# Attention and bilinear layers in split float32 on one core: the token-order softmax by VectorE block transposes and small DMAs in place of TensorE transposes, reads one batch later, state rows last

## The chip, the cores and the metric

The kernel runs on one core of a Trainium2 chip. The metric is the device time of one execution in microseconds. Before the change it is 510.85 us, the median of three runs (510.68 to 511.10). The engines are named as in the profile: PE is TensorE, DVE is VectorE, ACT is ScalarE, POOL is GpSimd, SP is SyncE (here it only issues DMAs).

## The reference, cut to what matters

```python
# x: 8 batches, 8 heads, 512 tokens, 64;  state: 8, 8, 32, 64
a  = softmax(x @ state.T / 8)          # each token over the 32 state rows
xread = a @ state
a2 = softmax(state @ x.T / 8)          # each state row over the 512 tokens
sread = a2 @ x
rows = concat(xread, sread)            # 544 rows a batch, 4352 in all, 512 wide
out = ((rows @ w1) * (rows @ w2)) @ w3 @ w_out
```

All of it is float32; the four weights come as float64. The layers have 1024 hidden columns.

## The kernel before, in words

**Precision.** A float32 operand of the large products is split into a rounded part and a remainder (`split`, lines 94 to 99: ACT writes `hi`, DVE subtracts and writes `lo`). A product is then three matmuls: hi by lo, hi by hi, lo by hi.

**Algebra.** w3 and w_out are multiplied once, in the prologue, to `wo` (line 85), eight column blocks (four in `w34_first`, 367, while the weights arrive; four in `w34(i)`, 379), each split by `finish(i)` (361). The token rows need no xread: the weights are multiplied with the state of a batch ("sets": `sw_steps`, 247; `sw_quarter`, 259, for batch 0), and stage 1 (281 to 295) multiplies these with the softmax `at`. Stage 1 has eight tiles `ft` of 128 hidden columns, 12 matmuls each; `hidden` (271) multiplies its two halves and splits the product into `g_hi` and `g_lo`. Stage 2 (304) multiplies g with `wo` for four token tiles `tt` of 128, 24 matmuls each, and `store` (312) copies the sum (ACT) and sends it out on ACT's DMA queue. Batch 0 does a part of stage 2 in between (`early_stage2`, 397).

**Softmax.** `attention_steps(b)` (160) has three parts. `scores` (164) computes `state @ x.T` in PSUM, 128 partitions by 1024; DVE transposes it in 32x32 blocks (172) and normalises over the state (to 202), and a second block transpose (206) gives `at`, which is split (208). The other softmax, over tokens, is the exponential `e2` (180 to 184) with its sums. `transpose_a2` (210) turns `e2` into token order with eight 128x128 transposes on PE (215) and a copy by ACT (217). `read_state` (219) multiplies that with the tokens `x_s` (64 matmuls by the profile's count, 227), DVE scales (232), and POOL's DMAs collect the rows in `sread` (237).

**Order.** PE's and SP's work runs as it is written; ACT's and DVE's is written by hand in the prologue up to `order.close()` (439), and set by a scheduler behind it. During the stage 2 of batch b stand the side steps of batch b+1 (`side_steps`, 319; `batch_stage2`, 342): scores and two sets behind the first token tile; transposes, two sets, reads and the rest of the softmax behind the second. Then `load_x(b + 2)` (145) loads state, `x_d` and the tokens `x_s`, the latter two into one buffer each. PSUM has two single banks for stage 2 and three pairs (`two_banks`, 91) for all else. At the start of batch 7 `state_rows` (480) does both stages for the 256 state rows, after `transpose_reads` (468) put `sread` into place during the last stage 2 of batch 6; the output of a state-row tile goes in four DMAs of 32 rows (501). A DMA from SP or ACT signals one of eight counters in turn, and waits until the DMA that had this counter before has landed.

Of the kernel before, what the change touches and what calls it, by code (L numbers as in the profile page):

```python
# [33 lines left out]
AHEAD = 2  # L34
PARTS = {0: (640, 1024), 1: (512, 1024)}
# [3 lines left out]
def attn_bilinear_kernel(  # L39
# [93 lines left out]
    x_tiles, sts = {}, {}  # L133
# [11 lines left out]
    def load_x(b):  # L145
        sts[b] = att.tile([P, NP, NS], F32, name="st")
        nc.sync.dma_start(out=sts[b], in_=st[b])
        x_tiles[b] = [
            att.tile([P, NP, S], F32, name="x_d", bufs=1), att.tile([P, NT, H, D], F32, name="x_s", bufs=1)
        ]  # L150
        for t, src in zip(x_tiles[b], (x_d, x_s)):
            nc.sync.dma_start(out=t, in_=src[b])
# [7 lines left out]
    def attention_steps(b):  # L160
        xd = x_tiles[b][0]
        a2 = {}

        def scores():
# [43 lines left out]
            split(*at_tiles[b], at)  # L208

        def transpose_a2():  # L210
            ps = two_banks()
            for kt in range(KT):
                for t in range(NT):
                    ts = slice(t * P, (t + 1) * P)
                    nc.tensor.transpose(out=ps[:, kt, ts], in_=a2["e"][:, kt, ts], identity=ident)  # L215
            a2["t"] = work_tile() if b < 2 else late.tile([P, KT, S], F32, name="a2_t")
            nc.scalar.copy(out=a2["t"], in_=ps)

        def read_state():

            xs = x_tiles[b][1]
# [19 lines left out]
        return scores, transpose_a2, read_state, a2  # L241
# [76 lines left out]

    def side_steps(b):

        if b == B:
            return [[]] * NT
        scores, transpose_a2, read_state, a2 = attention_steps(b)
        w = sw_steps(b)
        if b < 2:
            return [[scores, w[0], w[1]], [w[2], w[3], transpose_a2], [read_state], []]
        softmax = scores()
        first = partial(islice, softmax, 3)

        def rest():  # L330

            with tc.issue_after(a2["read"].ins):
                yield from softmax

        return [[first, w[0], w[1]], [transpose_a2, w[2], w[3], read_state, rest], [], []]
# [6 lines left out]
    def batch_stage2(b, gs):  # L342
        side = side_steps(b + 1)
        for tt in range(NT):

            between = transpose_reads if b == B - 2 and tt == NT - 1 else None
            stage2(gs, tt, [(out[b, tt * P:(tt + 1) * P], 0, P)], between)
            run(side[tt])
        if b + 2 < B:
# [3 lines left out]
    with tc.tile_pool(name="pro", bufs=2) as pro:  # L353
# [25 lines left out]
        def w34(i):  # L379
            w34_ps[i] = bank()  # L380
            for k in range(FT):
# [31 lines left out]
        scores, transpose_a2, read_state, _ = attention_steps(0)  # L413
        softmax = scores()
        next(softmax)
        for i in range(FT // 2):
            finish(i)
# [10 lines left out]
        transpose_a2()  # L428
# [127 lines left out]
```

## Time and profile before

| | |
|---|---|
| median of three runs | 510.85 us |
| profiled execution | 512.03 us |
| its span (first to last instruction) | 510.0 us |
| granted TensorE clock | 1.000 |
| transposes of the token softmax on PE (L215) | 64, 8.4 us busy |
| ACT copies behind them (L217) | 8, 1.01 us each |
| DMA, mean over the span | 95 GB/s |

The span is what the views divide; the profiled execution is 2.03 us longer than its span. A PE matmul of 128 by 512 is given with 390 to 397 ns, but matmuls overlap: a step from one to the next is 0.23 us. The chain of waits merges pieces of one engine and line, and so shows how long a group holds PE.

### The profile page before, as it was taken

What the parts mean: (1) busy time and instruction counts of PE and PEld (TensorE: products, weight loads), DVE (VectorE), ACT (ScalarE), POOL (GpSimd) and SP (SyncE); (2) the same over time, 40 slices, a digit from 0 to 9 for tenths busy, and PEclk for the clock granted to TensorE, in tenths of its full rate; (3) what the DMA queues carried; (4) which work ended last, traced back from release to release, by engine and by line L of the source; (5) the groups of instructions that cost most, each with busy time, mean ns of one, the idle gap of its engine ahead of it and who ended that gap; (6) DMA issues with size and microseconds to landing.
All of it is one profiled execution on the core that took longest, in us unless ns stands there. A gap on an engine that the chain in (4) does not pass through costs nothing.

```text
span 510.0 us, 7598 instructions
## 1 busy us (share of the span) xinstructions
PE 502.6 (99%) x3222; PEld 375.4 (74%) x3222; DVE 269.7 (53%) x370; ACT 227.6 (45%) x341; POOL 16.5 (3%) x38
## 2 busy tenths in 40 slices
PE   8999999999999999999999999999999999999997
PEld 6434457867876887688778867886788679998885
DVE  4669885466439253915391449154915583732510
ACT  6667784344436243624362435243524463632410
POOL 0000001001000100010001000000100010000000
PEclk9999999999999999999999999999999999999999
DMA  8997672032104300420042013201410001001001
GB/s 331 339 394 283 262 297 89 6 125 81 54 1 134 124 2 1 142 117 1 14 140 105 0 32 140 89 1 31 155 68 1 21 26 44 1 6 37 2 34 49
DMA packets 12386, 48.20 MB, mean 95 GB/s; under 512 B 1856, under 2 KB 3392, under 8 KB 7744
## 3 DMA queue, kind: packets, MB, share of 16 engines
q1 hardware_dynamic: 6336, 38.28, 20.6%
q10 hardware_dynamic: 4992, 8.92, 4.7%
q0 software_dynamic: 1024, 0.53, 0.4%
q8 instruction: 25, 0.41, 0.3%
q14 instruction: 9, 0.07, 0.1%
HBM read 38.27 MB, written 8.91 MB: 93 GB/s over the span
## 4 chain that ended last, share of the span: by engine, by line
PE 85%; DMA 6%; ACT 4%; DVE 3%; issue 1%; ACTq 0%; DVEq 0%
PE ps_o L300 37%; PE ps L290 34%; PE ps L141 7%; PE ps L494 5%; DMA raw<-in_w_k_dram 4%; ACT ulps L120 2%; PE ps L227 2%; DMA raw<-in_w3t_dram 1%; DMA raw<-in_w_dram 1%; PE ps L215 1%; ACT w_sb L117 1%; DVE wo_lo L98 1%; DVE w L128 0%; ACT w L117 0%; ACT wo_hi L97 0%
## 5 line engine op out<-in xcount | busy, mean ns | idle before, releaser
L300 PE MATMUL ps_o<-wo_lo,g_hi 128*128 128x512 f32 x272 | 107.9, 397 | 0.0
L300 PE MATMUL ps_o<-wo_hi,g_lo 128*128 128x512 f32 x272 | 106.1, 390 | 0.0
L300 PE MATMUL ps_o<-wo_hi,g_hi 128*128 128x512 f32 x272 | 105.9, 389 | 0.0
L275 DVE TENSOR_TENSOR tmp<-tmp,ps 128x512 f32<-128x512 f32 (+1 forms) x72 | 47.3, 656 | 107.4 <-ACT tmp L274 107.4
L290 PE MATMUL ps<-at_lo,sw_hi 128*128 128x512 f32 x256 | 100.1, 391 | 0.6 <-DVE sw_lo L98 0.6
L290 PE MATMUL ps<-at_hi,sw_hi 128*128 128x512 f32 x256 | 99.6, 389 | 0.0
L290 PE MATMUL ps<-at_hi,sw_lo 128*128 128x512 f32 x256 | 99.6, 389 | 0.0
L274 ACT COPY tmp<-ps 128x512 f32<-128x512 f32 (+1 forms) x72 | 40.5, 563 | 67.8 <-PE ps L290 66.9
L98 DVE TENSOR_TENSOR g_lo<-tmp,g_hi 128x512 fp32r<-128x512 f32 (+1 forms) x72 | 47.7, 662 | 42.8 <-ACT g_hi L97 42.7
L97 ACT CAST g_hi<-tmp 128x512 fp32r<-128x512 f32 (+1 forms) x72 | 42.9, 596 | 48.5 <-DVE tmp L275 48.4
L300 PEld LDWEIGHTS ps_o<-wo_lo,g_hi 128*128 128x128 f32 x272 | 51.0, 188 | 17.3 <-issue 6.7
L300 PEld LDWEIGHTS ps_o<-wo_hi,g_lo 128*128 128x128 f32 x272 | 51.1, 188 | 10.9
L315 ACT COPY tmp<-ps_o 128x512 f32<-128x512 f32 x34 | 20.0, 588 | 87.3 <-PE ps_o L300 87.3
L300 PEld LDWEIGHTS ps_o<-wo_hi,g_hi 128*128 128x128 f32 x272 | 51.1, 188 | 10.1
L290 PEld LDWEIGHTS ps<-at_lo,sw_hi 128*128 128x128 f32 x256 | 48.0, 188 | 11.5 <-DVE sw_lo L98 1.0
L290 PEld LDWEIGHTS ps<-at_hi,sw_lo 128*128 128x128 f32 x256 | 48.1, 188 | 10.0
L290 PEld LDWEIGHTS ps<-at_hi,sw_hi 128*128 128x128 f32 x256 | 48.1, 188 | 9.8
L98 DVE TENSOR_TENSOR sw_lo<-ps,sw_hi 128x1024 fp32r<-128x1024 f32 (+1 forms) x36 | 38.8, 1099 | 1.3 <-ACT sw_hi L97 0.2
L97 ACT CAST sw_hi<-ps 128x1024 fp32r<-128x1024 f32 (+1 forms) x36 | 32.2, 920 | 8.4 <-PE ps L141 8.3
L141 PE MATMUL ps<-w_sb,st 64*32 64x512 f32 (+1 forms) x576 | 31.5, 546 | 0.0
L237 POOL DMA_DIRECT2D sread<-scaled x32 | 15.8, 502 | 403.7 <-DVE scaled L232 403.7
L382 PE MATMUL ps_o<-w_sb,w 128*128 128x512 f32 x64 | 28.3, 597 | 0.5 <-DVE w L128 0.3
(65 smaller groups left out, 442.1 us busy)
## 6 DMA issues: line engine op xcount, KB each, us to landing
raw<-in_w_k_dram SPq DMA_DIRECT2D x8, 1024.0 KB, 6.9
x_d<-in_x_d_dram SPq DMA_DIRECT2D x8, 1024.0 KB, 5.4
x_s<-in_x_s_dram SPq DMA_DIRECT2D x8, 1024.0 KB, 5.7
raw<-in_w_dram SPq DMA_DIRECT2D x8, 1024.0 KB, 6.7
out_dram<-tmp ACTq DMA_DIRECT2D x32, 256.0 KB, 2.0
raw<-in_w3t_dram SPq DMA_DIRECT2D x4, 1024.0 KB, 7.5
st<-in_st_dram SPq DMA_DIRECT2D x8, 64.0 KB, 6.0
sread<-scaled POOLq DMA_DIRECT2D x32, 16.0 KB, 3.1
```

The source lines that it names most:

```text
L97: nc.scalar.copy(out=hi, in_=src),
L98: nc.vector.tensor_tensor(out=lo, in0=src, in1=hi.bitcast(F32), op=ALU.subtract),
L120: nc.scalar.activation(out=ulps[:, part], in_=low.bitcast(U32), func=AF.Copy, scale=2.0**-29)
L141: nc.tensor.matmul(ps[j * NS:(j + 1) * NS, q], sts[b][rows, j], moving(rows, j), start=True, stop=True)
L237: nc.gpsimd.dma_start(out=sread[rows, b // PER, j * KT:(j + 1) * KT], in_=scaled[j * NS:(j + 1) * NS])
L274: nc.scalar.copy(out=a_sb[:, :n], in_=ps[:, 0, :n])
L275: nc.vector.tensor_tensor(out=a_sb[:, :n], in0=a_sb[:, :n], in1=ps[:, 1, :n], op=ALU.mult)
L290: nc.tensor.matmul(ps[:, i], w[:, kt, c:c + P], a[:, kt], start=(k == 0), stop=(k == 3 * KT - 1))
L300: nc.tensor.matmul(ps[:, :DO], g, wo[w][:, ft, :], start=(ft == 0 and k == 0), stop=(ft == FT - 1 and k == 2))
L315: nc.scalar.copy(out=o, in_=ps[:, :DO])
L382: nc.tensor.matmul(w34_ps[i][:, :DO], w3s[i][:, k * P:(k + 1) * P], w_out[k], start=(k == 0), stop=(k == FT - 1))
L494: nc.tensor.matmul(ps[:, i, :n], w[:, ks], a, start=(k == 0), stop=(k == 3 * NP - 1))
```

## The change

The token softmax gets to token order without PE. At the end of the softmax (now a fourth part of `scores`) DVE transposes `e2` in 32x32 blocks, after the split of `at`, and SP issues 16 DMAs that put the blocks in their places: each takes 32 partitions, eight pieces of 32 numbers each. PE's eight transposes and ACT's copy go. The reads of batch b are done with the side steps of batch b+1 (those of batch 7 behind the first token tile of its own stage 2), and the tokens are loaded by a function of their own, `load_tokens`, at the end of the stage 2 before that. `transpose_reads` moves into the last stage 2 of batch 7, and the state rows behind everything. In the prologue, the columns 2 and 3 of w3 w_out are split in one piece; batch 0's tokens are loaded behind the third and fourth half of the weights; the second set stands inside the last column block of w3 w_out (five of eight matmuls before it, `LAST`, and three behind); and the scores of batch 1 come in the third quarter of batch 0's stage 1.

```diff
     def load_x(b):
...
-        x_tiles[b] = [
-            att.tile([P, NP, S], F32, name="x_d", bufs=1), att.tile([P, NT, H, D], F32, name="x_s", bufs=1)
-        ]
-        for t, src in zip(x_tiles[b], (x_d, x_s)):
-            nc.sync.dma_start(out=t, in_=src[b])
+        x_tiles[b] = att.tile([P, NP, S], F32, name="x_d", bufs=1)
+        nc.sync.dma_start(out=x_tiles[b], in_=x_d[b])
+
+    def load_tokens(b):
+        token_tiles[b] = att.tile([P, NT, H, D], F32, name="x_s", bufs=1)
+        nc.sync.dma_start(out=token_tiles[b], in_=x_s[b])
...
-            split(*at_tiles[b], at)
-
-        def transpose_a2():
-            ps = two_banks()
-            for kt in range(KT):
-                for t in range(NT):
-                    ts = slice(t * P, (t + 1) * P)
-                    nc.tensor.transpose(out=ps[:, kt, ts], in_=a2["e"][:, kt, ts], identity=ident)
+            last = split(*at_tiles[b], at)
+            yield
+
+            blocks = work_tile()
+            with tc.issue_after(last[1].ins):
+                nc.vector.transpose(out=flat(blocks), in_=flat(e2))
             a2["t"] = work_tile() if b < 2 else late.tile([P, KT, S], F32, name="a2_t")
-            nc.scalar.copy(out=a2["t"], in_=ps)
+            tiles = lambda t: t.rearrange("p k (t m) -> p (k t) m", m=P)
+            for j in range(NP):
+                for c in range(P // NS):
+                    mine, its = slice(j * NS, (j + 1) * NS), slice(c * NS, (c + 1) * NS)
+                    nc.sync.dma_start(out=tiles(a2["t"])[its, :, mine], in_=tiles(blocks)[mine, :, its])
...
         if b == B:
-            return [[]] * NT
-        scores, transpose_a2, read_state, a2 = attention_steps(b)
+            return [[reads[b - 1]], [], [], []]
+        scores, reads[b], a2 = attention_steps(b)
...
-        return [[first, w[0], w[1]], [transpose_a2, w[2], w[3], read_state, rest], [], []]
+        if b == 1:
+            return [[first], [reads[0], w[0], w[1]], [w[2], w[3], lambda: softmax], []]
+        return [[first, w[0], w[1]], [w[2], w[3], reads[b - 1], lambda: softmax], [], []]
...
-            between = transpose_reads if b == B - 2 and tt == NT - 1 else None
+            between = transpose_reads if b == B - 1 and tt == NT - 1 else None
...
+        if b + 1 < B:
+            load_tokens(b + 1)
         if b + 2 < B:
             load_x(b + 2)
...
-        for i in range(FT // 2):
-            finish(i)
+        finish(0)
+        finish(1)
+        split(wo["hi"][:, 2:4], wo["lo"][:, 2:4], pair[:, :, :DO])
...
-        transpose_a2()
...
+        load_tokens(0)
         w34(6)
         sets(0)
         finish(6)
-        w34(7)
+        w34(7, range(LAST))
+        sets(1)
+        w34(7, range(LAST, FT))
         finish(7)
-        sets(1)
...
-                load_x(1)
                 side = side_steps(1)
+            elif quarter == 2:
+                run(side.pop(0))
             stage1(0, 2 * quarter + 1, gs)
             if quarter == 0:
                 run([partial(convert_half, n) for n in range(4, 2 * QT)])
-                read_state()
-        run(side[0][1:] + side[0][:1])
+                load_x(1)
+                with tc.issue_after(last_split[1].ins):
+                    go(softmax)
+        run(side[0])
...
     for b in range(1, B):
-        if b == B - 1:
-            with tc.issue_after(last_split[0].ins), tc.issue_after(last_split[1].ins):
-                state_rows()
...
+    with tc.issue_after(last_split[0].ins), tc.issue_after(last_split[1].ins):
+        state_rows()
```

How the instructions stand, at three places. PE, the side steps of batch 3 behind the second token tile of batch 2 (L300 is stage 2, L215 the transposes, L141 a set, L227 the reads), before:

```order
L300 MATMUL ps_o<-wo_hi,g_lo 128x512
L215 MATMUL ps_1651<-ident,e_1582 128x128 x8
L141 MATMUL ps_1662<-w_sb,st 32x512 x8
L141 MATMUL ps_1675<-w_sb,st 32x512 x8
L227 MATMUL ps_1688<-x_s,a_t 32x64 x32
L300 MATMUL ps_o<-wo_lo,g_hi 128x512
```

And PE at the same place now (the lines are those of the changed kernel: L304 is stage 2, L142 a set, L231 the reads):

```order
L304 MATMUL ps_o<-wo_hi,g_lo 128x512
L142 MATMUL ps_1632<-w_sb,st 32x512 x8
L142 MATMUL ps_1645<-w_sb,st 32x512 x8
L231 MATMUL ps_1658<-x_s,a_t 32x64 x32
L304 MATMUL ps_o<-wo_lo,g_hi 128x512
```

The transposes are gone; the reads stand where they stood, but are those of batch 2. SP, from the last weights to the loads for batch 2, before:

```order
L113 DMA raw<-in_w_dram 128x1024 x6
L147 DMA st<-in_st_dram 128x128
L152 DMA x_d<-in_x_d_dram 128x2048
L152 DMA x_s<-in_x_s_dram 128x2048
L147 DMA st<-in_st_dram 128x128
```

And SP there now (L221 are the small DMAs, of batch 0 and batch 1 in one row):

```order
L114 DMA raw<-in_w_dram 128x1024 x2
L154 DMA x_s<-in_x_s_dram 128x2048
L114 DMA raw<-in_w_dram 128x1024 x4
L148 DMA st<-in_st_dram 128x128
L150 DMA x_d<-in_x_d_dram 128x2048
L221 DMA work<-work 32x8x32 x32
L154 DMA x_s<-in_x_s_dram 128x2048
```

Batch 0's tokens have moved behind two of the last six weight loads, and 32 small DMAs stand ahead of the tokens of batch 1. PE in the prologue, from the third column block of w3 w_out that is made there to stage 1 (L382 is w3 w_out, L290 stage 1), before:

```order
L215 MATMUL ps_317<-ident,e_271 128x128 x8
L382 MATMUL ps_o<-w_sb,w_260 128x512 x8
L141 MATMUL ps_365<-w_sb,st 32x256 x8
L141 MATMUL ps_378<-w_sb,st 32x256 x8
L382 MATMUL ps_o<-w_sb,w_332 128x512 x8
L141 MATMUL ps_402<-w_sb,st 32x256 x8
L141 MATMUL ps_413<-w_sb,st 32x256 x8
L290 MATMUL ps_425<-at_lo,sw_hi 128x512
```

And PE there now (L386 is w3 w_out, L294 stage 1):

```order
L386 MATMUL ps_o<-w_sb,w_256 128x512 x8
L142 MATMUL ps_352<-w_sb,st 32x256 x8
L142 MATMUL ps_365<-w_sb,st 32x256 x8
L386 MATMUL ps_o<-w_sb,w_317 128x512 x5
L142 MATMUL ps_384<-w_sb,st 32x256 x8
L142 MATMUL ps_395<-w_sb,st 32x256 x8
L386 MATMUL ps_o<-w_sb,w_317 128x512 x3
L294 MATMUL ps_412<-at_lo,sw_hi 128x512
```

The second set (ps_402 and ps_413, now ps_384 and ps_395) stands three matmuls earlier, inside the last column block.

More of the change, by code (lines that the diff above doesn't have):

```diff
@@ L34 @@
 AHEAD = 2
+LAST = 5
 PARTS = {0: (640, 1024), 1: (512, 1024)}
@@ L130, in to_f32 @@
                     )
-    x_tiles, sts = {}, {}
+    x_tiles, token_tiles, sts = {}, {}, {}
     def per_head(ps, b, moving):
@@ L160, in attention_steps @@
     def attention_steps(b):
-        xd = x_tiles[b][0]
+        xd = x_tiles[b]
         a2 = {}
@@ L239, in read_state @@
                 )
-        return scores, transpose_a2, read_state, a2
+        return scores, read_state, a2
     def sw_pair():
@@ L317, in store @@
             nc.scalar.dma_start(out=dest, in_=o[first:first + n])
+    reads = {}
     def side_steps(b):
         if b == B:
-            return [[]] * NT
-        scores, transpose_a2, read_state, a2 = attention_steps(b)
+            return [[reads[b - 1]], [], [], []]
+        scores, reads[b], a2 = attention_steps(b)
         w = sw_steps(b)
-        if b < 2:
-            return [[scores, w[0], w[1]], [w[2], w[3], transpose_a2], [read_state], []]
         softmax = scores()
         first = partial(islice, softmax, 3)
-        def rest():
-            with tc.issue_after(a2["read"].ins):
-                yield from softmax
-        return [[first, w[0], w[1]], [transpose_a2, w[2], w[3], read_state, rest], [], []]
+        if b == 1:
+            return [[first], [reads[0], w[0], w[1]], [w[2], w[3], lambda: softmax], []]
+        return [[first, w[0], w[1]], [w[2], w[3], reads[b - 1], lambda: softmax], [], []]
     def run(steps):
@@ L377, in convert_w3, with w34 @@
             return to_f32(pro, w3t[i - FT // 2], w3s[i])
-        def w34(i):
-            w34_ps[i] = bank()
-            for k in range(FT):
+        def w34(i, ks=range(FT)):
+            if ks[0] == 0:
+                w34_ps[i] = bank()
+            for k in ks:
                 nc.tensor.matmul(
@@ L412, in attn_bilinear_kernel @@
         load_x(0)
-        scores, transpose_a2, read_state, _ = attention_steps(0)
+        scores, reads[0], _ = attention_steps(0)
         softmax = scores()
         next(softmax)
-        for i in range(FT // 2):
-            finish(i)
+        finish(0)
+        finish(1)
+        split(wo["hi"][:, 2:4], wo["lo"][:, 2:4], pair[:, :, :DO])
         w34(4)
@@ L461, in attn_bilinear_kernel @@
                 run(side[tt - 1])
+        load_tokens(1)
         load_x(2)
```

2 lines of the change are left out of this document (1 added, 1 removed).

## The prediction

> **What bounds the kernel now.** The page's engine line and the shares of the chain that ended last come first: whose time is the span's time?
>
> ```profile
> PE 502.6 (99%) x3222; PEld 375.4 (74%) x3222; DVE 269.7 (53%) x370; ACT 227.6 (45%) x341; POOL 16.5 (3%) x38
> PE 85%; DMA 6%; ACT 4%; DVE 3%; issue 1%; ACTq 0%; DVEq 0%
> ```
>
> TensorE (PE) carries 85% of the chain; DMA, ScalarE and VectorE hold the other 14%, so I look where those lie. The view that gives busy time by stage (columns: length of the stage, then busy time of each engine) says it for the prologue, one batch in the middle and the tail.
>
> ```profile
> core 0: us, PE busy (x) PEld busy (x) DVE busy (x) ACT busy (x) POOL busy (x), PEclk, DMA share, GB/s
> 37.60:69.00 31.40, 31.02 (x136) 13.82 (x136) 28.52 (x37) 23.82 (x29) 0.00 (x0) 1.00 0.77 286
> 69.00:80.72 11.72, 11.15 (x141) 8.02 (x133) 9.53 (x15) 9.09 (x14) 0.89 (x2) 1.00 0.69 254
> 225.78:276.30 50.52, 50.52 (x345) 39.04 (x345) 26.04 (x34) 20.30 (x31) 1.97 (x4) 1.00 0.19 66
> 506.25:510.00 3.75, 0.00 (x0) 0.00 (x0) 0.00 (x0) 0.59 (x1) 0.00 (x0) 1.00 0.18 70
> ```
>
> In a middle batch PE is busy for 50.52 of 50.52 us, at full clock, while VectorE (DVE) is busy for 26.0 and ScalarE (ACT) for 20.3. So from the end of the prologue on, a microsecond taken off PE comes off the time, unless another engine then is late. In the prologue (37.6 to 69) DVE has 28.5 us of work in 31.4, as tight as PE. The tail is 3.75 us in which PE does nothing.
>
> **Term 1: the transposes on PE.** The chain in order of time (start, length, what) lists them in every batch; first, third and last of the seven after batch 0, with their neighbours in the third.
>
> ```profile
> 116.95 1.02 PE ps L215 x8
> ...
> 205.19 5.68 PE ps_o L300 x24
> 210.87 0.87 PE ps L215 x8
> 211.74 1.88 PE ps L141 x32
> 213.62 1.03 PE ps L227 x64
> 214.65 11.13 PE ps_o L300 x48
> ...
> 412.97 0.87 PE ps L215 x8
> ```
>
> The pieces follow without a gap, and the next piece is PE's in any case, so removing eight transposes removes their 0.87 us. Six batches give 5.22 and batch 1 gives 1.02: **6.24 us off**. All eight reads of the state remain, at 1.03 us each, and only change places; the pieces that begin alone after a switch of shape are as many as before (reads of batches 0 and 1 stood alone, now the scores of batch 1 and the reads of batch 7), so moving them costs nothing net.
>
> The transposes come at 109 ns each here (0.87 over 8). The Trainium skill ("TensorE: Matmul & The Clock Gate", Part 4: PE-mode transpose) gives about 275 ns for one in a kernel's context, and the page "VectorE: DVE Perf Modes" (The three transpose paths, and its rules) says to keep 128x128 transposes on TensorE. By 275 ns the estimate for 56 transposes would be 15.4 us off; the chain's row decides for 6.24.
>
> **What must take their place.** DVE does one more block transpose a batch, ACT one copy less.
>
> ```profile
> L206 DVE STREAM_TRANSPOSE work<-work 128x1024 f32<-128x1024 f32 x8 | 9.9, 1236 | 0.0
> L217 ACT COPY a_t<-ps 128x1024 f32<-128x1024 f32 x6 | 6.1, 1012 | 2.5 <-PE ps L215 2.5
> 218.73 1.23 DVE L98 TENSOR_TENSOR at_lo<-work,at_hi 128x1024 fp32r<-128x1024 f32 x1 [1.11 <-ACT at_hi L97]
> 229.15 0.69 DVE L275 TENSOR_TENSOR tmp<-tmp,ps 128x512 f32<-128x512 f32 x1 [9.20 <-ACT tmp L274]
> ```
>
> The new transpose has the form of L206, 1.24 us, and stands right behind the at_lo split; the last two rows show that DVE then idles for 9.2 us. It is covered eightfold; without that cover it would be 1.24 us a batch.
>
> Behind it SP issues 16 DMAs of 32 partitions x 8 pieces of 128 bytes (32 KB each). No row shows such a DMA. The nearest:
>
> ```profile
> 214.71 0.33 SPq L152 DMA_DIRECT2D x_s<-in_x_s_dram  x1
> 215.09 0.42 SPq L147 DMA_DIRECT2D st<-in_st_dram  x1
> sread<-scaled POOLq DMA_DIRECT2D x32, 16.0 KB, 3.1
> out_dram<-tmp ACTq DMA_DIRECT2D x8, 64.0 KB, 1.7
> ```
>
> SP issues one per 0.38 us (214.71 to 215.09), so 16 take 6.1 us; the landing lies between 1.7 us (rows of 2 KB) and 3.1 us (rows of 512 bytes). I take 3.1, nearest in size of piece: all 16 are in after 6.1 + 3.1 = **9.2 us**. The lower end is 7.8; the upper end is that they don't overlap at all, 16 x 3.1 = 50.
>
> Who waits? The reads, on PE, come a batch later, some 40 us on: no wait. The loads behind them on SP (tokens, then the next x_d) are needed a batch later too. Two places are closer.
> - Batch 0: its 16 DMAs read the work buffer into which DVE puts the scores of batch 1. DVE, and with it the splits that stage 1 needs, stands behind that wait. The pieces of PE between lengths it can hide in:
>
> ```profile
> 80.72 2.94 PE ps_o L300 x12
> 83.66 5.44 PE ps L290 x24
> 89.10 1.02 PE ps L141 x32
> 90.13 2.94 PE ps_o L300 x12
> ```
>
>  These four, 12.34 us, and 0.87 for the scores give 13.2 us from the last split of the first quarter to the scores; 1.24 goes to the block transpose, leaving 12.0. PE itself stalls only when the scores' PSUM buffer is wanted again, three tiles of stage 1 later; since the softmax needs most of that, I allow 1 us for it: **13 us against 9.2**, so nothing. If it takes the 50 us of the upper end, 37.
> - Every batch: the output DMA of the fourth token tile, on ACT, takes a completion counter that the fifth small DMA held, and ACT's first copy of the next stage 1 (L274, for which DVE waits in the last row of the softmax above) is behind it. The fifth is due 5 x 0.38 + 3.1 = 5 us after 221.2, at 226.2, about when that output is ready. A tile of stage 1 is 2.72 us (the 24 matmuls in 5.44 above are two tiles), and with three PSUM pairs the fourth tile wants the first one's back at 225.78 - 0.87 + 8.16 = 233.1; less a copy and a product, ACT must go on by 231.5. So PE would notice only from 10 us on. Nothing again.
>
> **Term 2: the prologue.** The pieces of it that end last, on PE, DVE and ACT:
>
> ```profile
> 38.86 0.59 ACT L97 CAST wo_hi<-ps 128x512 fp32r<-128x512 f32 x1 [1.64 <-DVE wo_lo L98]
> 39.47 0.69 DVE L98 TENSOR_TENSOR wo_lo<-ps,wo_hi 128x512 fp32r<-128x512 f32 x1 [0.65 <-ACT wo_hi L97]
> 40.08 1.24 DVE L172 STREAM_TRANSPOSE work<-ps 128x1024 f32<-128x1024 f32 x1
> 41.18 1.15 ACT L117 ACTIVATE w_sb<-raw 128x1024 f32<-128x1024 f32 x1 [1.73 <-DMA raw<-in_w_dram]
> 51.52 1.04 PE L215 MATMUL ps<-ident,e 128*128 128x128 f32 x8
> 52.85 1.12 PE L382 MATMUL ps_o<-w_sb,w 128*128 128x512 f32 x2 [0.30 <-DVE w L128]
> 71.66 0.39 PE L290 MATMUL ps<-at_hi,sw_lo 128*128 128x512 f32 x1
> 72.61 0.50 PE L290 MATMUL ps<-at_lo,sw_hi 128*128 128x512 f32 x1 [0.57 <-DVE sw_lo L98]
> 74.15 1.14 ACT L117 ACTIVATE w_sb<-raw 128x1024 f32<-128x1024 f32 x1 [1.13 <-DMA raw<-in_w_dram]
> ```
>
> The transposes of batch 0 (1.04 us) are worth nothing by themselves: after them PE waits 0.30 us more for the converted w3 from DVE. What moves that conversion is the split of w3 w_out's columns 2 and 3. It was two pairs with a wait between (ACT 1.64, DVE 0.65 idle); in one piece of 1024 the subtraction starts at once, at 38.14, and with the 1.23 of the at_lo row ends at 39.37 instead of 40.08. DVE has hardly a gap from there to 52.85, so w3 w_out continues **0.7 us earlier**. ACT must keep up: its weights (landed at 41.18) come sooner, because the 1 MB of tokens no longer stands ahead of them on SP, and it loses a copy of 1.0 us.
>
> Next, stage 1's second tile waits from 71.89 (71.66 and one step of 0.23) to 72.61 for the split of the second set, because a PSUM pair isn't free: with that set inside w3 w_out its split comes some 2.5 us earlier, and the 0.72 and 0.1 of restart go. **0.8 us off**, less **0.2** for one more switch of shape. What is late next is the last weights' landing (74.15), then ACT's and DVE's work of the first quarter; two more copies than before stand ahead of the first g there, and DVE has the block transpose besides. I count 1.3 us off in all, between 0 and 2.
>
> **Term 3: the end.** State rows end with four DMAs for a tile, batch 7 ended with one.
>
> ```profile
> 457.93 1.77 ACTq L317 DMA_DIRECT2D out_dram<-tmp  x4
> 506.89 0.34 ACTq L317 DMA_DIRECT2D out_dram<-tmp  x1
> out_dram<-tmp ACTq DMA_DIRECT2D x32, 256.0 KB, 2.0
> ```
>
> The last is issued 1.77 - 0.34 = 1.43 us later and lands in 1.7 instead of 2.0: **1.1 us more** (0.3 if issue overlaps landing fully). PE's state rows are the same work at another place, and the transposes of the reads have the same three steps of stage 2 behind them as before, which cover their splits.
>
> **Sum.** -6.24 - 1.3 + 1.1 = -6.4 us. The profile's span is 510.0 us, its execution 512.03; the three plain runs have a median of 510.85. I put the difference on the median: **504.4 us**. About 0.2% (1 us) is what a measurement of this kernel can tell from no change.
>
> **The rivals.**
> - *A stall appears in the first quarter* (0.18). The 16 DMAs of batch 0 take 16 us rather than 9, or ACT and DVE are late after the last weights: 3 us of PE time, once. For it: 69 to 80.72 is the one stretch after 37.6 with PE idle beside busy ACT and DVE. Time: 507.4.
> - *The small DMAs run one behind the other* (0.08). Then the count is 16 times a landing. Break-even is where batch 0's DMAs take 13 + 6.4 = 19.4 us, 1.2 us each; at 2.0 us each they take 32, DVE holds PE for 19 us, and the fifth one in the other batches, at 10 us, just costs nothing: 510.85 - 6.4 + 19 = 523. Against it: the eight completion counters let eight be in flight, and the stage 37.6 to 69 moves 286 GB/s with several loads in flight. The Trainium skill speaks for it ("DMA: Bandwidth & Descriptors", Anatomy of one DMA and Rules for kernel authors): a DMA costs about 2.0 us and its bytes over 436 GB/s, and below 64 KB it is mostly overhead, so coalesce; an estimate from it is 2.08 us each and 33 us in a row, 524.
> - *Nothing comes of it* (0.05): the PE time returns as waits, 510.5. That needs the next batch's at_lo to be late; at 219.96 it ends 5.8 us before stage 1 starts at 225.78, and 0.87 is taken from those. Unlikely.
> - *More than the sum* (0.07): both ends of the prologue and the tail on the good side, -8.5: 502.3.
> - The forecast keeps 0.62.
>
> **Range and chances.** Leaving out the slower rival (0.08) and some of the other ends, 502.2 to 508.4 holds 8 in 10: the forecast, the larger gain and the stall up to 4 us. Faster: 0.62 + 0.18 + 0.07 = 0.87; same 0.05; slower 0.08.
>
> **What would show it.** Right: the chain has no L215, a middle batch lasts 49.65 us instead of 50.52 with PE busy throughout; stage 1's second tile starts without a wait; the last PE work ends some 4.8 us before the span does. Wrong: a wait of DVE's scores transpose of batch 1 for DMAs with PE idle around it; small DMAs that land in over 1.2 us times their number; a wait of ACT for an output DMA before L274's copy.

## The result, and the profile after

The changed kernel takes 505.19 us, the median of four runs (504.76 to 506.46), beside 510.98 us for the kernel before on the same chip: 5.8 us less. The ratio is 0.9891, with a 95% interval of 0.9875 to 0.9906. I had forecast 504.4, between 502.2 and 508.4.

The profiled run took 504.76 us, its span is 502.8; the profile of before shows 512.03 and 510.0. The spans differ by 7.2 us and the medians by 5.8, since the profiled run of before was one of its slower ones: the runs of one kernel spread over 2 us and more. So differences below one microsecond are read from medians, and traces only tell where time lies.

The page of the changed kernel has these two lines on the engines and on the chain of waits.

```profile
PE 495.3 (99%) x3158; PEld 367.6 (73%) x3158; DVE 278.2 (55%) x377; ACT 219.7 (44%) x332; POOL 16.5 (3%) x38
PE 93%; ACT 3%; DVE 2%; DMA 1%; issue 0%; DVEq 0%; ACTq 0%
```

PE has 64 instructions and 7.3 us less, and carries 93% of the chain where it carried 85%: in this trace PE bounds the kernel more than before. In a second trace of the changed kernel, further down, the chain runs through the small DMAs of batch 0 and PE has 84% of it, as before: at that place two chains of nearly the same length meet. The stages (length, then busy time by engine, granted clock, DMA) and the chain through one middle batch:

```profile
220.00:269.62 49.62, 49.62 (x338) 38.10 (x337) 27.17 (x35) 19.31 (x31) 1.96 (x4) 1.00 0.26 78
497.94:502.80 4.86, 0.00 (x0) 0.00 (x0) 0.00 (x0) 0.58 (x1) 0.00 (x0) 0.78 0.20 54
```

```profile
170.22 21.76 PE ps L294 x96
...
200.15 5.67 PE ps_o L304 x24
205.82 1.88 PE ps L142 x32
207.70 1.03 PE ps L231 x64
208.73 11.11 PE ps_o L304 x48
219.84 21.76 PE ps L294 x96
```

From one stage 1 to the next pass 219.84 - 170.22 = 49.62 us, where it was 50.52. The eight transposes that stood between the 24 matmuls of stage 2 and the 32 of the sets are gone, the reads of the state (L231, 1.03) are where they were, now for the batch before, and no piece waits. The price is on the other engines: DVE 1.1 us more a batch, ACT 1.0 less. The tail is 4.86 us instead of 3.75.

Before batch 1 two things are new. The first rows are of the DMA issues and the waits (engine, line, releaser, sum, times, longest); the small DMAs are those into `a_t` and from `work` to `work`. Then, from the order of time: SP's 16 issues for batch 0, DVE's next scores, and PE's one stall.

```profile
a_t<-work SPq DMA_DIRECT2D x96, 32.0 KB, 1.9
work<-work SPq DMA_DIRECT2D x32, 32.0 KB, 1.9
ACT tmp L278 <- DMA a_t<-work: 4.4, 4, 2.1
```

```profile
77.87 10.96 SPq L221 DMA_DIRECT2D work<-work  x16
90.22 1.25 DVE L174 STREAM_TRANSPOSE work<-ps 128x1024 f32<-128x1024 f32 x1 [1.82 <-DMA work<-work]
107.32 0.50 PE L304 MATMUL ps_o<-wo_lo,g_hi 128*128 128x512 f32 x1 [0.34 <-ACT tmp L319]
```

Sixteen issues take 10.96 us, 0.69 each with the waits between, and a DMA lands in 1.9 us. DVE waits 1.82 us for the last one before it takes batch 1's scores, as the rival of a stall in the first quarter had it, but in this trace PE does not stall there. It stalls at 107.32, for an output copy on ACT. Which of the two causes that stall the experiments had to tell.

### The profile page after: what moved, and what is told of

Same layout as the page of the kernel before. It is cut to its first block, busy times and chain, and to the rows that moved or that the text cites. A ratio compares the mean times of both kernels' runs of the same rounds, so it can differ in the third digit from the quotient of the medians.

```text
span 502.8 us, 7697 instructions
## 1 busy us (share of the span) xinstructions
PE 495.3 (99%) x3158; PEld 367.6 (73%) x3158; DVE 278.2 (55%) x377; ACT 219.7 (44%) x332; POOL 16.5 (3%) x38
## 4 chain that ended last, share of the span: by engine, by line
PE 93%; ACT 3%; DVE 2%; DMA 1%; issue 0%; DVEq 0%; ACTq 0%
PE ps_o L304 37%; PE ps L294 35%; PE ps L142 7%; PE ps L504 5%; PE ps_o L386 3%; PE ps_o L373 3%; PE ps L373 3%; PE ps L231 1%; DMA raw<-in_w_k_dram 1%; ACT ulps L121 1%; ACT w_sb L118 0%; ACT sw_hi L98 0%; ACT wo_hi L98 0%; DVE w L129 0%; DVE work L192 0%; DVE wo_lo L99 0%
## 5 line engine op out<-in xcount | busy, mean ns | idle before, releaser
L304 PE MATMUL ps_o<-wo_lo,g_hi 128*128 128x512 f32 x272 | 108.0, 397 | 0.3 <-ACT tmp L319 0.3
L304 PE MATMUL ps_o<-wo_hi,g_hi 128*128 128x512 f32 x272 | 106.0, 390 | 0.0
L304 PE MATMUL ps_o<-wo_hi,g_lo 128*128 128x512 f32 x272 | 106.0, 390 | 0.0
L294 PE MATMUL ps<-at_lo,sw_hi 128*128 128x512 f32 x256 | 100.1, 391 | 0.0
L294 PE MATMUL ps<-at_hi,sw_lo 128*128 128x512 f32 x256 | 99.6, 389 | 0.0
L294 PE MATMUL ps<-at_hi,sw_hi 128*128 128x512 f32 x256 | 99.6, 389 | 0.0
L304 PEld LDWEIGHTS ps_o<-wo_lo,g_hi 128*128 128x128 f32 x272 | 51.0, 188 | 18.9 <-issue 7.1
L304 PEld LDWEIGHTS ps_o<-wo_hi,g_lo 128*128 128x128 f32 x272 | 51.0, 188 | 10.9
L304 PEld LDWEIGHTS ps_o<-wo_hi,g_hi 128*128 128x128 f32 x272 | 51.1, 188 | 10.0
L294 PEld LDWEIGHTS ps<-at_lo,sw_hi 128*128 128x128 f32 x256 | 48.0, 188 | 10.9 <-issue 1.1
L294 PEld LDWEIGHTS ps<-at_hi,sw_hi 128*128 128x128 f32 x256 | 48.1, 188 | 10.2 <-issue 0.2
L294 PEld LDWEIGHTS ps<-at_hi,sw_lo 128*128 128x128 f32 x256 | 48.0, 188 | 10.0
L142 PE MATMUL ps<-w_sb,st 64*32 64x512 f32 (+1 forms) x576 | 31.5, 546 | 0.0
L386 PE MATMUL ps_o<-w_sb,w 128*128 128x512 f32 x64 | 28.5, 599 | 0.1
```

What stands on the lines that cost most here:

```text
L142: nc.tensor.matmul(ps[j * NS:(j + 1) * NS, q], sts[b][rows, j], moving(rows, j), start=True, stop=True)
L294: nc.tensor.matmul(ps[:, i], w[:, kt, c:c + P], a[:, kt], start=(k == 0), stop=(k == 3 * KT - 1))
L304: nc.tensor.matmul(ps[:, :DO], g, wo[w][:, ft, :], start=(ft == 0 and k == 0), stop=(ft == FT - 1 and k == 2))
L386: nc.tensor.matmul(w34_ps[i][:, :DO], w3s[i][:, k * P:(k + 1) * P], w_out[k], start=(k == 0), stop=(k == FT - 1))
```

## The experiments

The theory: the gain is PE's own time in the transposes; the small DMAs are covered; the prologue brings 1.3 us and the tail takes 1.1. The rivals: the small DMAs cost PE something in the first quarter, or the gain is not the transposes' but comes from the reads being later and the rows last. Each kernel was timed beside the kernel before.

### The kernel before, once more

> The kernel before, unchanged, as a second trace and a measure of what a repetition alone moves. The theory of the prediction (PE's transposes, the prologue, the tail) expects no difference in time, within 0.2%, but a prologue that starts stage 1 at 67.5 to 69.5 us: the 1.6 us by which it started earlier in the changed kernel (67.41 against 69.03) is then 0.9 of chance in the first weight loads and 0.7 of the split in one piece. The rival, that the prologue's edits brought all 1.6, expects 69.0 again.

Measured: 510.85 us (510.27 to 514.27, 12 runs), ratio 1.0006 (0.9991 to 1.0021). Its fastest and slowest runs lie 4 us apart, but its median and that of the 23 runs beside it (510.91) agree within 0.1. In its trace stage 1 starts at 69.30 us, which lies in the theory's range and near the rival's value, and the traced run, at 512.19 us, is one of the slower ones again: how much of the earlier start is chance stays open.

### All transposes back on PE, at the place of the small DMAs

```diff
-            blocks = work_tile()
-            with tc.issue_after(last[1].ins):
-                nc.vector.transpose(out=flat(blocks), in_=flat(e2))
+            ps = two_banks()
+            for kt in range(KT):
+                for t in range(NT):
+                    ts = slice(t * P, (t + 1) * P)
+                    nc.tensor.transpose(out=ps[:, kt, ts], in_=e2[:, kt, ts], identity=ident)
...
-            for j in range(NP):
-                for c in range(P // NS):
-                    mine, its = slice(j * NS, (j + 1) * NS), slice(c * NS, (c + 1) * NS)
-                    nc.sync.dma_start(out=tiles(a2["t"])[its, :, mine], in_=tiles(blocks)[mine, :, its])
+            nc.scalar.copy(out=a2["t"], in_=ps)
```

> The changed kernel with the token softmax turned round on PE again (eight transposes into PSUM, a copy by ACT), at the end of the softmax where DVE's block transpose and the 16 DMAs were; reads a batch later, state rows last and the prologue stay. The theory: eight times 0.87 to 1.02 us of PE come back, 7.0 to 8.0 us on the changed kernel, 512 to 513 us in all, that is slower than the kernel before by 1 to 2 us, since what it keeps of the change is a prologue worth 1.3 and a tail that costs 1.1. The rival (the new order of the work is what gained, and PE's transposes fitted into waits): at most 2 us on the changed kernel, 507.

Measured: 534.92 us (533.52 to 536.92, 5 runs), ratio 1.0472 (1.0451 to 1.0493): 29.7 us over the changed kernel, four times what the theory gave. Its trace shows that this is the experiment's own fault. First PE's rows in the order of time at a middle batch, then the stages around (the number behind POOL's is the granted clock).

```profile
216.71 1.30 PE L217 MATMUL ps<-ident,e 128*128 128x128 f32 x8 [2.51 <-DVE sw_lo L99]
...
218.23 0.63 PE L302 MATMUL ps_o<-wo_hi,g_hi 128*128 128x512 f32 x1
218.66 0.63 PE L302 MATMUL ps_o<-wo_hi,g_lo 128*128 128x512 f32 x1
...
221.30 0.39 PE L302 MATMUL ps_o<-wo_lo,g_hi 128*128 128x512 f32 x1
221.53 0.39 PE L302 MATMUL ps_o<-wo_hi,g_hi 128*128 128x512 f32 x1
```

```profile
216.71:218.01 1.30, 1.30 (x9) 1.30 (x10) 1.30 (x2) 0.82 (x1) 0.00 (x0) 0.78 1.03 435
218.01:230.30 12.29, 12.29 (x49) 10.00 (x49) 1.20 (x2) 1.60 (x2) 1.96 (x4) 0.88 0.33 130
```

At that place the transposes want a PSUM pair that DVE still has to split, so PE waits 2.51 us in each of the last five batches, and afterwards the clock is lower: matmuls that follow each other every 0.23 us (221.30 to 221.53) come every 0.43 us (218.23 to 218.66) for three microseconds. The 48 matmuls take 12.29 us instead of 11.11, the transposes 1.30 instead of 0.87. Together 2.51 + 1.30 + 1.18 make 5.0 us a batch, 25 in the five batches. The first of the six that have this order waits only 1.26 us, keeps its clock and loses 2.2, and 3.3 us more have gone before the stage 1 of batch 1 starts (at 123.90 instead of 120.60): that makes the 30. The experiment says nothing of the change; it was made again, below.

### The prologue's edits alone, in the kernel before

```diff
-        for i in range(FT // 2):
-            finish(i)
+        finish(0)
+        finish(1)
+        split(wo["hi"][:, 2:4], wo["lo"][:, 2:4], pair[:, :, :DO])
...
+        load_tokens(0)
         w34(6)
...
-        w34(7)
+        w34(7, range(LAST))
+        sets(1)
+        w34(7, range(LAST, FT))
         finish(7)
-        sets(1)
```

> The kernel before with the three edits of the prologue alone: the split of columns 2 and 3 in one piece, batch 0's tokens loaded behind the fourth half of the weights, the second set inside the last column block of w3 w_out. The theory: 0.7 of the split and 0.8 of the wait at stage 1's second tile, less 0.2: 1.3 us off, 509.5 us. The rival (the prologue gained 2.8 us, as the two traces stand side by side): 508.1.

Measured: 511.26 us (510.37 to 513.56, 12 runs), ratio 1.0004 (0.9992 to 1.0017). Both were wrong: alone, the edits bring nothing, and a gain of more than 0.4 us lies outside the interval. Stage 1 does start earlier in the trace, at 67.9, but PE then waits 0.97 us for a product of DVE (at 75.30), where the changed kernel has no wait. The trace had looked better (a span of 508.7), but it is of one of the four fastest of twelve.

### Half of the state rows' output on another queue

```diff
-        for dest, first, n in dests:
-            nc.scalar.dma_start(out=dest, in_=o[first:first + n])
+        for k, (dest, first, n) in enumerate(dests):
+            (nc.sync if k % 2 else nc.scalar).dma_start(out=dest, in_=o[first:first + n])
```

> The changed kernel with every second of a state-row tile's four output DMAs on SP's queue. The theory: the tail is four issues of 0.44 us on one queue and a landing; with two on each queue the last is issued 0.9 us earlier, 504.3 us against 505.2, and the span ends 4.0 us after PE's last work instead of 4.9. The rival (the last landing overlaps the issues, or the four share one engine row): no difference within 0.2 us.

Measured: 504.33 us (504.12 to 506.37, 5 runs), ratio 0.9881 (0.9865 to 0.9897); the changed kernel has 505.2 and 0.9891 (0.9875 to 0.9906). The intervals overlap, so that the 0.9 us are not shown by the times alone. The end of the changed kernel, and of this one:

```profile
497.96 0.58 ACT L319 COPY tmp<-ps_o 128x512 f32<-128x512 f32 x1 [4.85 <-PE ps_o L304]
498.58 1.76 ACTq L321 DMA_DIRECT2D out_dram<-tmp  x4
```

```profile
498.68 0.78 SPq L321 DMA_DIRECT2D out_dram<-tmp  x2
498.69 0.85 ACTq L321 DMA_DIRECT2D out_dram<-tmp  x2
```

Four issues on one queue are 1.76 us behind the last copy; two on each are 0.85, and the span ends 4.25 us behind PE's last work (498.05) instead of 4.86. So the issues were most of the tail's growth, and in the trace 0.6 of its 1.1 us can be had back.

### All transposes back on PE, where they had stood

The transposes of batches 2 to 7 stand ahead of the third set, those of batch 1 behind its softmax, those of batch 0 in the prologue; `a_t` has two buffers; reads one batch later, rows last and the prologue's edits stay. One line of the edit:

```diff
-        return [[first, w[0], w[1]], [w[2], w[3], reads[b - 1], lambda: softmax], [], []]
+        return [[first, w[0], w[1]], [transpose_a2, w[2], w[3], reads[b - 1], lambda: softmax], [], []]
```

> The changed kernel with the transposes of all batches back on TensorE (and ScalarE's copy out of PSUM), each at the place where the kernel before had it: in batches 2 to 7 ahead of the third set of w products, in batch 0 inside the prologue, in batch 1 behind its softmax. No small DMAs, no third block transpose. Reads one batch later, state rows last and the prologue's edits stay. Theory (the gain is the transposes' PE time and nothing else; the earlier 29.7 us were that experiment's own stall and the clock that fell behind it): 6.2 us more than the changed kernel, less the 0.5 us of stall that its small DMAs may cause in the first quarter, 510.9 to 511.5; a middle batch of 50.5 us at full clock. Rival A (transposes on TensorE pull the clock down wherever they stand in this order): a batch over 52 us, over 520. Rival B (the gain comes from the reads being later and the rows last): at most 507.

Measured: 513.35 us (512.66 to 514.70, 6 runs), ratio 1.0046 (1.0028 to 1.0063): slower even than the kernel before. Rivals A and B are out. The chain at a middle batch:

```profile
174.62 21.76 PE ps L292 x96
...
210.24 0.87 PE ps L217 x8
211.12 1.88 PE ps L142 x32
...
225.15 21.76 PE ps L292 x96
```

From stage 1 to stage 1 pass 50.53 us again, with the transposes' 0.87 in it and the matmuls at their old pace. So the transposes of a middle batch cost what I had counted. But 8.1 us over the changed kernel is 2 us more than the theory, and the trace puts them ahead of the first stage 2, which starts at 79.24 instead of 76.64. That made batch 0 the next question.

### Batch 0's transposes alone back on PE

```diff
+            if b:
...
+            else:
+                turned = two_banks()
+                for kt in range(KT):
+                    for t in range(NT):
+                        ts = slice(t * P, (t + 1) * P)
+                        nc.tensor.transpose(out=turned[:, kt, ts], in_=e2[:, kt, ts], identity=ident)
...
+            if b == 0:
+                nc.scalar.copy(out=a2["t"], in_=turned)
+                return
```

With this the step is called in the prologue, behind the sixth column block of w3 w_out, and no longer in the first quarter.

> The changed kernel with the transposes of batch 0 alone back on TensorE, inside the prologue where the kernel before had them, with ScalarE's copy out of PSUM behind them; batches 1 to 7 keep block transposes and small DMAs. Theory (in the prologue the copy of 1.0 us on ScalarE delays the conversion of the weights behind it, and that costs more than the transposes' own time; the first quarter's wait for the small DMAs was covered): 2 to 2.5 us more than the changed kernel, 507.2 to 507.7, the first tile's copy out of PSUM 1.5 us later. Rival (the transposes fall into a wait of TensorE, as I predicted, and the 0.5 us stall of the first quarter goes with the small DMAs): 504.5 to 505.2.

Measured: 507.28 us (506.83 to 507.37, 5 runs), ratio 0.9928 (0.9915 to 0.9940), beside 505.22 for the changed kernel on the same chip: 2.06 us for 1.04 us of PE work of which I had said that it was worth nothing. The rows of this kernel are on ACT, then PE.

```profile
74.17 0.56 ACT L288 COPY tmp<-ps 128x512 f32<-128x512 f32 x1
76.34 0.62 ACT L98 CAST g_hi<-tmp 128x512 fp32r<-128x512 f32 x1 [1.61 <-DVE tmp L289]
76.87 0.58 ACT L288 COPY tmp<-ps 128x512 f32<-128x512 f32 x1
...
78.34 0.67 PE L142 MATMUL ps<-w_sb,st 64*32 64x256 f32 x16 [1.22 <-DVE tmp L289]
```

And the changed kernel's ACT at the same place:

```profile
72.67 1.07 ACT L278 COPY tmp<-ps 128x512 f32<-128x512 f32 x2
74.74 1.22 ACT L98 CAST g_hi<-tmp 128x512 fp32r<-128x512 f32 x2 [1.00 <-DVE tmp L279]
```

Two things differ. ACT comes 1.5 us later to the first tile's copy (74.17 against 72.67; with all transposes in place, where the first loads came as early as in the changed kernel, it is 74.29): it has a copy of 1.0 us more to do, and the weights' conversions, whose buffers the next loads wait for, stand behind it. (In this trace 0.7 us of lateness stand before the transposes already: DVE's conversion of w3 starts at 49.55 against 48.86.) And it takes the first two tiles in turn: copy, cast, copy, cast, waiting 1.61 us for DVE's product between, while in the changed kernel both copies stand ahead of both casts. In turn, the second tile's PSUM pair comes back late, and PE waits 1.22 us for it. ACT's order there is the scheduler's, behind the part written by hand. In the other kernels the orders go with the times: copies in turn in the kernel before, in that with the prologue's edits alone, in that with all transposes in place and in this one; both copies first in the changed kernel and in the two below that are as fast or faster (the second set back, the two edits more). The rows speak for the order: DVE's product of the first tile starts at 75.63 here, and if that of the second stood right behind it, as in the changed kernel, it would end at 76.9, before PE wants the pair at 77.1. By that the 1.22 us are the order's. But the order was not changed by itself, so what it costs apart from the later start is not shown.

### The prologue's edits undone in the changed kernel

The diff of the prologue's edits above, the other way round.

> The changed kernel with its three edits of the prologue undone: tokens of batch 0 loaded right behind x_d, the split of w3 w_out's columns 2 and 3 in two pairs, and the second set of w products behind w3 w_out. Theory (the stages' starts in the two traces tell the truth, the prologue's term is real): 1.3 to 2.0 us more, 506.5 to 507.2, and stage 1's second tile waits some 0.7 us again. Rival (what the prologue gains is lost again before batch 1, or lies within the jitter of the first loads, as when these edits were made alone): 505.0 to 505.5.

Measured: 507.38 us (506.01 to 509.04, 6 runs), ratio 0.9929 (0.9908 to 0.9949): 2.2 us more, just over the theory's upper end, though the same edits alone had brought nothing. Rows of DVE, and PE's stall:

```profile
78.20 1.24 DVE L215 STREAM_TRANSPOSE work<-e 128x1024 f32<-128x1024 f32 x1
...
92.55 1.25 DVE L174 STREAM_TRANSPOSE work<-ps 128x1024 f32<-128x1024 f32 x1 [3.14 <-DMA work<-work]
...
98.49 0.50 PE L304 MATMUL ps_o<-wo_hi,g_lo 128*128 128x512 f32 x1 [0.42 <-DVE g_lo L99]
```

The copies come in turn here too, the second at 75.49 (at 73.14 where only the second set is back). The block transpose behind them starts 1.6 us later than in the changed kernel, the small DMAs end 13.2 us behind it (79.36 to 92.55), DVE waits 3.14 us for them, and now PE does feel it, by 0.42 us. In the changed kernel it was 12.4 us (77.77 to 90.22) and no wait of PE. But its second trace (of the repetition further down) has 13.2 us too (77.72 to 90.94): SP takes 11.72 us for the 16 issues there, DVE waits 2.62 us for the last landing, and the matmul that wants DVE's split (at 96.87) comes 0.52 us behind the one before it and not 0.23. The chain of waits of that trace goes this way:

```profile
88.93 1.92 DMA work<-work
...
90.94 1.25 DVE work L174
...
96.87 1.90 PE ps_o L304 x7
```

So the small DMAs of batch 0 use up their cover in the changed kernel already, and PE loses between nothing and 0.3 us by them. The edits do not add up: with batch 0's copy on ACT, adding them changes nothing; without it, taking them away costs 2.2 us.

### One of the three: the second set behind w3 w_out again

```diff
-        w34(7, range(LAST))
-        sets(1)
-        w34(7, range(LAST, FT))
+        w34(7)
         finish(7)
+        sets(1)
```

> The changed kernel with one edit of the prologue undone: the second set of w products stands behind the last w3 w_out again, and not inside it. Theory (my prediction's term: 0.8 us off for the second tile's wait, 0.2 on for the switch of shape): 0.6 us more, 505.8. Rival A (the split of the second set also held up the block transpose and its small DMAs, and so the first quarter): 1.2 us more or over, 506.4 or more. Rival B (the last weights' conversion ends last in either order): 505.2.

Measured: 505.05 us (504.98 to 505.16, 4 runs), ratio 0.9886 (0.9873 to 0.9900), beside 505.22: nothing, so rival B. Stage 1's first tiles in its chain:

```profile
67.06 2.99 PE ps L294 x12
70.08 5.74 PE ps L294 x24
```

Three tiles take 2.99 + 5.74 us here and 8.20 in the changed kernel, 0.5 more; the matmuls of w3 w_out ahead of them, in one piece, take 7.06 and not 4.49 + 2.77, 0.2 less. The wait of 0.72 us that I had read in the profile of before is not there without the other edits undone.

### The small DMAs twice, in batch 0

```diff
-            for j in range(NP):
+            for j in list(range(NP)) * (2 if b == 0 else 1):
```

> The changed kernel with the 16 small DMAs of batch 0 issued twice over (32, the second time the same data to the same place). 16 more issues at 0.61 us are 9.8 us. Theory (they end last in the first quarter: VectorE's scores transpose of batch 1 waits for them and PE has at most some 1.5 us of cover left): that transpose waits 11.6 us instead of 1.8, PE stalls by 8 to 10 us, 513 to 515. Rival (the 0.5 us of PE stall there has another cause, ACT's copies, and the PSUM pair is wanted later than I counted): less than 509.

Measured: 510.74 us (509.52 to 511.92, 12 runs), ratio 0.9984 (0.9967 to 1.0002): 5.5 us more, between the two. SP's issues and DVE's rows at the scores transpose, then PE behind it, then the stage that follows:

```profile
77.88 22.06 SPq L221 DMA_DIRECT2D work<-work  x32
...
101.85 0.69 DVE L279 TENSOR_TENSOR tmp<-tmp,ps 128x512 f32<-128x512 f32 x1 [3.37 <-ACT tmp L278]
102.45 1.24 DVE L174 STREAM_TRANSPOSE work<-ps 128x1024 f32<-128x1024 f32 x1
```

```profile
106.85 1.09 PE L142 MATMUL ps<-w_sb,st 64*32 64x512 f32 x16 [3.17 <-DVE scaled L236]
```

```profile
107.95:117.92 9.97, 9.97 (x44) 7.82 (x51) 8.75 (x11) 4.21 (x7) 1.25 (x3) 0.83 0.17 61
```

This is not the stall as the theory meant it. SP issues until 99.9, and the DMAs move data until 100.9, so that DVE's transpose could not have come before some 101 in any order. No wait for a DMA stands before it, since in this kernel the scheduler put it behind the products of stage 1's last three tiles; it comes at 102.45, 12.2 us later than in the changed kernel. What the order spares is those products: they no longer stand behind the transpose, and PE has them in time; this is read from the rows and not tested. The softmax then comes late, PE waits 3.17 us, and the 36 matmuls behind run at a clock of 0.83 and take 9.97 us for 8.38. So 16 more small DMAs do cost, a third of a microsecond for each, but in an order that doubling changed too; the cover in the changed kernel's own order is read from the kernel above (12.4 us free, 13.2 not). The stall at 107.32 had yet to be explained.

### The small DMAs twice, in the other batches

```diff
-            for j in range(NP):
+            for j in list(range(NP)) * (2 if b else 1):
```

> The changed kernel with the 16 small DMAs of batches 1 to 7 issued twice over, batch 0's once. Theory (a batch later is far enough: 9.8 us more on SP's queue per batch hide): 505.0 to 505.6, a middle batch of 49.6 us. Rival (the output DMA of the fourth token tile, or ACT behind it, takes a completion counter that a small DMA holds, and stage 1 waits; or more DMAs slow PE's own reads of memory): at least 1 us a batch, 511 or more.

Measured: 505.14 us (505.06 to 505.77, 4 runs), ratio 0.9885 (0.9867 to 0.9904). The theory holds: 112 DMAs more cost nothing. The chain has the same middle batch:

```profile
170.92 21.76 PE ps L294 x96
...
209.43 11.11 PE ps_o L304 x48
220.54 21.76 PE ps L294 x96
```

220.54 - 170.92 is 49.62 us again. ACT's waits for output DMAs or small DMAs ahead of its first copy (2.1 us the longest, in both kernels) lie under PE's work, as predicted.

### The changed kernel again, and with two edits more

```diff
-            nc.scalar.copy(out=o, in_=ps[:, :DO])
+            stores.append(nc.scalar.copy(out=o, in_=ps[:, :DO]))
...
+            def rest():
+                with tc.issue_after(stores[1].ins):
+                    yield from softmax
-            return [[first], [reads[0], w[0], w[1]], [w[2], w[3], lambda: softmax], []]
+            return [[first], [reads[0], w[0], w[1]], [w[2], w[3], rest], []]
```

The edit of the two queues goes with it.

> The changed kernel as it is, for a comparison on one chip with the three beside it. Both theories: 505.2, between 504.8 and 505.6.

> The changed kernel with two edits: every second output DMA of a state-row tile on SP's queue instead of ScalarE's, and batch 1's transposed scores (block transpose, split) held until the second token tile of batch 0 has been copied out, so that on ScalarE the copies for the two sets of w products and the two output copies stand ahead of that split. Theory (the 0.5 us stall of TensorE behind the first output copy comes from the order on ScalarE, not from the small DMAs, and the four issues of the last tile are the tail): 0.6 and 0.5 us off, 503.9 to 504.3, no wait of stage 2 for an output copy. Rival (the stall belongs to the small DMAs' wait on VectorE): 504.4 to 504.6, the stall still there.

Measured: the changed kernel 505.22 us (504.83 to 506.10), ratio 0.9893 (0.9876 to 0.9910); with the two edits 503.68 us (503.54 to 505.02), ratio 0.9865 (0.9850 to 0.9881): 1.5 us less, a little more than the 1.1 expected, and the fastest of all. ACT before batch 0's output copies, first of the changed kernel, then with the edits:

```profile
103.91 1.05 ACT L98 CAST at_hi<-work 128x1024 fp32r<-128x1024 f32 x1 [0.73 <-DVE work L208]
104.86 1.92 ACT L98 CAST sw_hi<-ps 128x1024 fp32r<-128x1024 f32 x2
106.67 0.60 ACT L319 COPY tmp<-ps_o 128x512 f32<-128x512 f32 x1
```

```profile
103.45 1.93 ACT L98 CAST sw_hi<-ps 128x1024 fp32r<-128x1024 f32 x2
105.88 0.59 ACT L319 COPY tmp<-ps_o 128x512 f32<-128x512 f32 x1 [0.50 <-PE ps_o L304]
...
107.67 1.05 ACT L98 CAST at_hi<-work 128x1024 fp32r<-128x1024 f32 x1
```

In the changed kernel ACT goes from one task to the next, and PE waits for the copy; with the edits ACT waits 0.50 us for PE, and no wait of PE is left in this stretch. The stall was made by the place of `at_hi` on ACT, not by the small DMAs: the kernel with batch 0's transposes on PE, where batch 0 has no small DMAs, has the same wait, and so has that with all of them on PE (0.34 us at 109.92).

```profile
109.69 0.50 PE L314 MATMUL ps_o<-wo_lo,g_hi 128*128 128x512 f32 x1 [0.34 <-ACT tmp L329]
```

## Why the prediction was right, and where it was not

The forecast was 504.4 and the result 505.2; the sum was -6.4 and is -5.8. The direction and the main term came by the mechanism that was forecast. That the total came so near is in part luck: the prologue gave some 0.8 us more than I had counted, and two costs that the sum did not have (0.5 and some 0.7 us, below) took that back and a little more.

- **Term 1, the transposes of batches 1 to 7: right.** -6.24 by the chain; the kernel with them in place, less that with batch 0's alone, is 513.35 - 507.28 = 6.07 us (on two chips; by the ratios, 1.0046 and 0.9928, it is 6.0), and a batch is 0.90 us shorter. Reads that only move cost nothing in a middle batch: 1.03 us before and after. The 275 ns that the prediction quotes for a transpose are the length of one, 272 to 273 ns in the trace of before too; they overlap, and 109 ns from one to the next is what eight of them hold PE.
- **Term 2, the prologue: the step that failed.** "The transposes of batch 0 (1.04 us) are worth nothing by themselves" was true of PE's microsecond and wrong of what came with it: ACT's copy of 1.0 us, which I had named only as a help. The exchange for block transpose and small DMAs, without that copy, is worth 2.06 us. The edits I had priced at 1.3 together bring nothing alone, and the 0.8 - 0.2 for the second set are 0 (505.22 against 505.05). I had added up ends of pieces as if they were independent, where ACT, DVE and the scheduler's order decide together. How much of the 2 us is the later start and how much the order of ACT's copies stays open; the rows give the order 1.2 of them.
- **Term 3, the tail: right.** +1.1 in the trace (4.86 against 3.75); two queues give 0.6 us of it back in the trace.
- **The small DMAs: right in their cover, wrong in their price, and so nearly wrong in what they cost.** An issue takes 0.69 us with its waits and not 0.38, a landing 1.9 and not 3.1, together 12.4 us instead of 9.2. Against 13 us of cover that was still nothing, by half a microsecond; at the 13.2 us of the second trace PE came 0.3 us late, and at those of the kernel with the prologue undone it waited 0.42. The rows of plain loads were a poor price for the issue of a DMA with 256 pieces.
- **The rivals.** DMAs one behind the other would have taken 16 x 1.9 = 30 us, and took 12.4, since they overlap. The Trainium skill ("DMA: Bandwidth & Descriptors", Anatomy of one DMA and Rules for kernel authors) gives, for a DMA from GpSimd, 2.0 us and its bytes over 436 GB/s, by an estimate 2.08 for 32 KB, and the 1.9 of these DMAs from SP are near it; it advises to coalesce, since below 64 KB a DMA is mostly overhead, and here 112 more of them, for which nobody waited, cost nothing. The stall of 3 us in the first quarter did not appear. What did is the 0.3 us above, in one of two traces, and 0.5 us later on from another cause: `at_hi` ahead of an output copy on ACT, in a place I had not looked at.
- **A term that I had put at nothing.** -6.0, -2.1, +1.1 for the tail and +0.5 for the stall make -6.5, against -5.8 and -5.4 in two comparisons. Most of the rest is in the chains of the two traces. From batch 0's first piece of stage 2 to the stage 1 of batch 1 pass 43.96 us (76.64 to 120.60) where it was 43.78 (80.72 to 124.50), though the 1.02 of the transposes are gone and PE's other work there is the same. These 1.2 us are the stall's 0.5 and some 0.7 of the new order. Some 0.4 of that can be named: the scores of batch 1, which stood with two sets (2.74 for the three), now stand alone (1.02, and the sets 1.88), and the 24 matmuls of stage 1 behind them take 5.68 instead of 5.44. So my "moving them costs nothing net" was wrong by some 0.7. With it the sum is -5.8; no run took this order back alone.

The signs of being right came as said: no transposes in the chain, 49.62 us for a batch (49.65 said), three tiles of stage 1 without a wait, 4.86 us behind the last PE work (4.8 said). Two of the signs of being wrong came in part: DVE's scores transpose waited 1.82 and 2.62 us for the small DMAs, with PE late by 0.3 us at most, and ACT waited up to 2.1 us for an output DMA ahead of its first copy, under PE's work. So as signs they were too strict.

## What to carry to other kernels

Where one engine carries the chain without a gap, work taken off it is worth its own length, and the slow path that replaces it (here the 112 small DMAs of batches 1 to 7) is free as long as its result is due a batch later; test that by doubling it, and see that the doubling has not changed the order of other work. Where three engines share the bound, as in a prologue, a copy or an order on the engine beside can count for more than the work that was moved, and edits need not add up: try them alone and together. Before putting work back to test a change, look what it will wait for at its new place.

## What the runs showed of the hardware

**A short idle lowers PE's clock.** Behind 2.51 us of waiting and eight transposes matmuls came half as fast for three microseconds (steps of 0.43 us instead of 0.23, granted clock 0.52 from 218.01 to 221.00); behind a wait of 3.17 us in the kernel with batch 0's DMAs doubled they did so too (0.52 from 107.90 to 111.30; 0.83 on average over 9.97 us, 1.6 us lost). A wait of 1.22 us, in the kernel with batch 0 on PE, left no such mark: the twelve matmuls behind it took 2.94 us, as ever. Nor did one of 1.26 us with eight transposes behind it: the 48 matmuls that followed took 10.92 us. The Trainium skill ("TensorE: Matmul & The Clock Gate", Part 1) says that the clock falls to half after an idle window of some 3.4 us, and (Part 4) that transposes do not count as busy in the same way; by the two, 2.51 and 1.30 us make up to 3.8 us of idle, and the rows agree, with a granted clock of 0.65 in the last 0.81 us of the transposes. The 3.17 us are a little less than the 3.4; no run here shows what besides them counted. So a stall of PE has two prices, and the second came here to half of the first or more (1.6 us behind 2.51 and behind 3.17).

**An issue on SP is dearer for a scattered DMA.** A DMA of 32 partitions with eight pieces each held SP for 0.61 us in the median, and plain loads of the kernel before 0.33 (`x_d`, `x_s`) and 0.43 (`st`). For 16 in a row it is the issue, not the landing, that counts: 10.96 of the 12.4 us.
